# A fused attention and feed-forward kernel in fp32: first product by Strassen, one more product by two levels, a new order of the first two batches, and a list schedule of its own

## The chip, the cores and the metric

The kernel runs on one core of a Trainium2 chip. The metric is the device time of one execution in microseconds (us). The engines that matter here are TensorE (PE in the profile: matrix products into PSUM), VectorE (DVE), ScalarE (ACT), GpSimd (POOL[...]) and the DMA queues, most of which are fed by SyncE (SP). Every engine works through its own list of instructions in order and waits for others by semaphores.

## The reference, cut to what matters

There are 8 batches with 8 heads, 512 tokens and 32 state rows of width 64. Tokens attend to the state rows and the state rows to the tokens; both results together form 544 rows of width 512 per batch. They go through two matrix products with an ELU between them. The weights come in as float64.

```python
B, H, S, Ns, D = (8, 8, 512, 32, 64)
scores = scale * np.matmul(x, state.transpose(0, 1, 3, 2))      # tokens x state
a = softmax(scores);   xread = np.matmul(a, state)
scores2 = scale * np.matmul(state, x.transpose(0, 1, 3, 2))     # state x tokens
a2 = softmax(scores2); sread = np.matmul(a2, x)
...
h = x @ w_in                                                    # 512 -> 2048
g = np.where(h > 0.0, h, alpha * (np.exp(np.minimum(h, 0.0)) - 1.0))
return (g @ w_out).astype(np.float32)                           # 2048 -> 512
```

The kernel does not form `xread`. For a batch it forms m = (state rows times w_in), 256 x 2048, and then h = a m, so that the "first product" of a batch has an inner size of 256 instead of 512. The "second product" is g times w_out. The 256 state rows of all batches go through plain w_in at the end.

## The kernel before: the parts that matter

A batch's first product, plain: per block of 128 hidden columns two calls of 512 columns, then the ELU by two passes on ACT and one on DVE.

```python
def ffn1(b, fo):
    ps = bank(4 + fo % 2 if b == 0 else 3 + (fo + 1) % 3)
    for k in range(G):                       # G = 2
        matmul(ps, m_t[b, fo // 4][:, k, fo % 4 * P : (fo % 4 + 1) * P], st[b, k, "aT"],
               start=(k == 0), stop=(k == G - 1))
    return ps

def exp_part(ps):
    e = epool.tile([P, ps.shape[-1]], FP32, tag="e", name="e_sb")
    scalar.activation(out=e, in_=ps, func=AF.Relu, scale=-1.0)
    scalar.activation(out=e, in_=e, func=AF.Exp, scale=-1.0)
    return e

def max_part(fo, e, ps):                     # max(e - 1, h)
    vector.scalar_tensor_tensor(out=g_all[:, fo, : ps.shape[-1]], in0=e, scalar=-1.0, in1=ps,
                                op0=ALU.add, op1=ALU.max)
```

m is made by small matmuls on tiles of the array (64 rows, 32 columns each), 8 calls of 512 columns per chunk of 512 hidden columns; in batch 0 in halves of 256 columns.

The second product is done by Strassen's method (in Winograd's form: 7 products, here called P1 to P7, of blocks of half size) in batches 1 to 7 and for the state rows; P3, P4, P5 and P7 are again done so inside ("two levels", class `Second`) in batches 2 to 7, and P3 and P4 in batch 1. Batch 0 does it plainly.

```python
def ffn2_row(ps, fo):                        # batch 0
    for c in range(R):                       # R = 4
        matmul(ps[c], g_all[:, fo, c * P : (c + 1) * P], w_out[:, fo],
               start=(fo == 0), stop=(fo == FO - 1))
...
# class Strassen, steps(); two = self.second
product(0, self.a11, b11, after_p1, first=True)
product(1, self.a12, b21, after_p2, first=True, last=True)
product(0, self.s, t_w[2], after_p6, last=5 in two)          # P6, one level
if 7 in two:
    in_two(7, 2, (1, 1), after_p7, fresh=True)
...
used = {k: second[k] for k in (4, 3)}        # batch 1
```

The weights are converted from raw float64 words in 32 blocks, each by 3 passes on ACT and 4 on DVE. A written-out plan for batch 0 interleaves, block by block, the conversion of w_in, the conversion of w_out, the first product (`F`), the ELU (`R`, `E`) and the second product (`O`), and fills TensorE's early holes with products that nothing reads (`Z`):

```python
w:8.1 Z:8 sr:0 tt:0.0 src:0 w:2.2 Z:14 F:0 w:6.1 F:1 w:8.2 R:0 M:0.0.1 R:1 E:0 Mc:0.0.1
E:1 O:0 w:9.1 w:4.2 w:10.1 w:9.2 F:2 w:7.1 w:6.2 M:0.1.0 F:3 R:2 w:7.2 Mc:0.1.0 O:1
...
```

Of the kernel before, what the change touches and what calls it, by code (L numbers as in the profile page):

```python
# [17 lines left out]


# [3 lines left out]


@with_exitstack
def kernel(
# [8 lines left out]

# [14 lines left out]
    NRAW = 7  # L53
# [8 lines left out]
    w_in_v = moe_w_in.rearrange("(co ci) f -> ci co f", ci=P)  # L62
    w_out_v = moe_w_out.rearrange("(fo fi) c -> fi fo c", fi=P)

    def pool(name, bufs, **kw):
        return ctx.enter_context(tc.tile_pool(name=name, bufs=bufs, **kw))

    cpool = pool("const", 1)
    xpool = pool("x", 1)
    apool = pool("attn", 2)  # L70
    atpool = pool("aT", 2)
    mpool = pool("m", 3)
    work = pool("work", NRAW + 4)
    small = pool("small", 4)
    epool = pool("elu", 3)
    opool = pool("o", 2)
    wpool = pool("w2", 1)


    w_in_mem = pool("mem", 1, space=bass.MemoryType.DRAM).tile(  # L80
        [P, 2 * FC, NP, 256], FP32, name="w_in_mem"
    )
    psum = pool("ps", 1, space=PSUM).tile([P, 8, 512], FP32, name="ps")

    def bank(i):
        return psum[:, i]

    def pair(i):

        return psum[:, i : i + 2]  # L90

    class InOrder:
        def __init__(self, engine):
            self.engine, self.on = engine, True

        def __getattr__(self, name):
            def call(*args, **kw):
                ins = getattr(self.engine, name)(*args, **kw)  # L100
                return tc.keep_in_program_order(ins) if self.on else ins

            return call

    tensor, sync, vector, scalar, gpsimd = (
        InOrder(e) for e in (nc.tensor, nc.sync, nc.vector, nc.scalar, nc.gpsimd)
    )
    matmul = tensor.matmul

    def transpose(out, in_):  # L110


        for t in range(2):
            rows = slice(t * 64, (t + 1) * 64)
            tensor.transpose(out[:, t], in_[rows], ident[rows, rows], tile_position=(t * 64, 0))
# [4 lines left out]
    ident = cpool.tile([P, P], FP32, name="ident")  # L120

    w_in = cpool.tile([P, 2 * FC, NP, 256], FP32, name="w_in")
    w_out = cpool.tile([P, FO, DM], FP32, name="w_out")

    g_all = cpool.tile([P, FO, S], FP32, name="g_all")

    kT = cpool.tile([P, B, P], FP32, name="kT")

    read = cpool.tile([P, B, G, D], FP32, name="read")

    x_t, st, m_t = {}, {}, {}

    def load_x(b, engines):
        x_t[b] = xpool.tile([P, R, DM], FP32, name="x_sb")
        x_v = x[b].rearrange("h (p r) d -> p r h d", r=R)
        for r in range(R):
            engines[r % len(engines)].dma_start(
                out=x_t[b][:, r].rearrange("p (h d) -> p h d", d=D), in_=x_v[:, r]
            )

    def load_blocks(b):

        for i in range(2):
            st[b, "blocks", i] = raw = opool.tile([P, 2, R * P], FP32, tag="o", name="x_blocks")
            for j in range(2):
                for k in range(4):
                    x_v = x[b, 2 * (2 * i + j) + k // 2].rearrange(
                        "(q p r) d -> p r q d", q=P // 32, r=R  # L150
                    )
                    sync.dma_start(
                        out=raw[k * 32 : (k + 1) * 32, j].rearrange(
                            "p (r q d) -> p r q d", r=R, d=32
                        ),
                        in_=x_v[:, :, :, k % 2 * 32 : (k % 2 + 1) * 32],
                    )

    def turn_blocks(b, m):

        i, j = divmod(m, 2)
        if j == 0:
            st[b, "xT", i] = work.tile([P, 2, R * P], FP32, tag="w", name="xT_b")
        st[b, m] = st[b, "xT", i][:, j]
        vector.transpose(st[b, m], st[b, "blocks", i][:, j])

    state_v = state.rearrange("b (m c) n d -> c m n b d", c=G)

    def load_states(b0, b1, engines=None):

        shape = [P, b1 - b0, G, D]
        if b0 == 0:
            raw = cpool.tile(shape, FP32, name="s_first")
        else:
            raw = work.tile(shape, FP32, tag="w", name="s_sb")
        for c in range(G):
            if b0 == 0:
                engines[c % len(engines)].dma_start(out=raw[:, 0, c], in_=state_v[c, :, :, 0])
                continue
            for m in range(NP):  # L180
                sync.dma_start(
                    out=raw[m * NS : (m + 1) * NS, :, c], in_=state_v[c, m, :, b0:b1]
                )
        return raw

    def turn_states(raw, b0, b1):
        ps = st["k_ps"] = pair(6)[:, :, : (b1 - b0) * 64].rearrange("p t (b q) -> p t b q", q=64)
        for b in range(b1 - b0):
            transpose(ps[:, :, b], raw[:, b].rearrange("p c d -> p (c d)"))

    def copy_states(b0, b1):
        vector.tensor_copy(
            out=kT[:, b0:b1].rearrange("p b (t q) -> p t b q", t=2), in_=st["k_ps"]
        )

    def load_weights(src):
        _, n, k = src.shape
        raw = work.tile([P, n, k], moe_w_in.dtype, tag="w", name="raw")
        sync.dma_start(out=raw, in_=src)
        return raw  # L200

    def low_words(raw):
        return raw.bitcast(U32).rearrange("p n (j w) -> p n j w", w=2)[:, :, :, 0]

    def high_words(raw):
        return raw.bitcast(U32).rearrange("p n (j w) -> p n j w", w=2)[:, :, :, 1]

    def convert_1(dst, raw):

        lo, hi = low_words(raw), high_words(raw)

        scalar.activation(
            out=lo.bitcast(FP32), in_=lo, func=AF.Copy, scale=2.0**-29, bias=2.0**23
        )
        scalar.activation(out=lo, in_=lo.bitcast(FP32), func=AF.Copy, bias=-(2.0**23))


        scalar.activation(out=dst, in_=hi.bitcast(FP32), func=AF.Abs)  # L220

    def convert_2(dst, raw):
        lo, hi = low_words(raw), high_words(raw)
        vector.tensor_scalar(
            out=dst, in0=dst, scalar1=as_float(896 << 20),
            scalar2=as_float((1151 << 20) - 1), op0=ALU.max, op1=ALU.min,
        )

        bits = dst.bitcast(U32)
        vector.tensor_scalar(  # L230
            out=bits, in0=bits, scalar1=3, scalar2=0x3FFFFFF8,
            op0=ALU.logical_shift_left, op1=ALU.bitwise_and,
        )
        vector.scalar_tensor_tensor(
            out=bits, in0=hi, scalar=0xC0000000, in1=bits,
            op0=ALU.bitwise_and, op1=ALU.bitwise_or,
        )
        vector.tensor_tensor(out=bits, in0=bits, in1=lo, op=ALU.add)

    def load_w_in(c, k):  # L240

        h, n = divmod(k, 2)
        rows = slice(2 * n, 2 * n + 2)
        cols = slice(c * 512 + h * 256, c * 512 + (h + 1) * 256)
        return w_in[:, 2 * c + h, rows], load_weights(w_in_v[:, rows, cols])

    def load_w_out(fo):
        raw = load_weights(w_out_v[:, fo : fo + 1])
        return w_out[:, fo : fo + 1], raw

    def turn_x(b, i, first=6):

        ps = pair(first).rearrange("p t (j r q) -> p t j r q", j=2, q=64)
        for j in range(2):
            for r in range(R):
                m = 2 * i + j
                transpose(ps[:, :, j, r], x_t[b][:, r, m * P : (m + 1) * P])
        st[b, "xT", i] = ps

    def copy_x(b, i):  # L260
        xT = opool.tile([P, 2, R * P], FP32, tag="o", name="xT")
        for j in range(2):
            st[b, 2 * i + j] = xT[:, j]
            scalar.copy(
                out=xT[:, j].rearrange("p (r t q) -> p t r q", t=2, q=64),
                in_=st[b, "xT", i][:, :, j],
            )

    def by_state(b, rhs, first=6):


        ps = pair(first)
        _, j, n = rhs[0].shape
        for m in range(NP):
            for g in range(G):
                d = slice(g * D, (g + 1) * D)
                matmul(
                    ps[m * NS : (m + 1) * NS, g, : j * n].rearrange("p (j n) -> p j n", j=j),
                    kT[d, b, m * NS : (m + 1) * NS],
                    rhs[m][d],  # L280
                    start=True,
# [291 lines left out]

# [160 lines left out]

# [202 lines left out]
```

## Time and profile before

Three runs gave 747.8, 748.39 and 748.39 us, median 748.39. The profiled execution spans 744.4 us, at a granted TensorE clock of 1.000.

| What | Value |
|---|---|
| Start of batch 2 on TensorE | 213.84 us |
| Batches 2 to 6, each | about 79.6 us |
| Batch 7 (611.8 to 689.0) | 77.2 us |
| State rows to the end (689.0 to 744.4) | 55.4 us |
| POOL TENSOR_TENSOR, 128x512 | 1047 to 1063 ns each |
| ACT first pass of the ELU, 128x512 (from PSUM) | 597 ns each |
| DVE last pass of the ELU, 128x512 | 685 ns each |
| First matmul of a first product | 31.96 us |

In the profile a matmul call shows as two records. A line of the timeline gives the start, the length until the last of the group has ended, the engine, and the group of equal instructions; the next group may start before the last one has ended, so a rate is read from start to start. In the table of stretches the columns are the stretch, its length, the busy time and the number of instructions of PE, weight load, DVE, ACT and POOL, the granted clock, the DMA share and GB/s.

### The profile page before, as it was taken

The numbers are of one execution on the slowest core, as the hardware profiler recorded it, in microseconds if no ns is written. First come the engines' busy times: TensorE is split into PE (matmuls) and PEld (weight loads), VectorE is DVE, ScalarE is ACT, GpSimd is POOL, SyncE is SP. The second block draws the span as 40 slices with busy tenths as digits, with TensorE's granted clock in tenths as the row PEclk, the third lists the DMA queues.
The fourth block names the chain that finished last, engine by engine and source line by source line (L and its number), as shares of the span: only waits on it lengthen the run. The fifth ranks groups of instructions, "written<-read, shape, count | busy, mean of one in ns | idle before, by whom it ended". The sixth has DMA issues, their size and how long they took to land.

```text
span 744.4 us, 11377 instructions
## 1 busy us (share of the span) xinstructions
PE 723.7 (97%) x4472; PEld 502.5 (68%) x4472; DVE 486.0 (65%) x892; ACT 293.3 (39%) x539; POOL 34.4 (5%) x38
## 2 busy tenths in 40 slices
PE   4899999989999999999999999999999999999998
PEld 2544444348874798469944896479746894699886
DVE  2999975799437883677556864787367845556231
ACT  5899955542126311651055203621264106400420
POOL 0100002002000200010000200020002000000000
PEclk9999999999999999999999999999999999999999
DMA  9667900801634063503461164307340403003000
GB/s 282 225 201 239 326 0 1 167 4 22 177 94 133 5 179 84 160 1 106 122 153 46 26 173 110 116 13 187 83 144 1 143 33 137 1 1 142 29 4 25
DMA packets 126366, 76.25 MB, mean 102 GB/s; under 512 B 113768, under 2 KB 114280, under 8 KB 122472
## 3 DMA queue, kind: packets, MB, share of 16 engines
q1 hardware_dynamic: 124004, 74.90, 34.8%
q10 hardware_dynamic: 2308, 0.62, 0.4%
q8 instruction: 35, 0.57, 0.3%
q14 instruction: 19, 0.16, 0.1%
HBM read 59.24 MB, written 13.11 MB: 97 GB/s over the span
## 4 chain that ended last, share of the span: by engine, by line
PE 89%; DVE 6%; SPq 1%; DMA 1%; ACT 1%; issue 1%; POOL 0%; ACTq 0%; DVEq 0%; POOLq 0%
PE ps L100 89%; DVE w_in L100 2%; SPq L100 1%; DMA x_sb<-in_x_dram 1%; DVE g_all L100 1%; DVE total_t L100 0%; DVE s L100 0%; DVE top L100 0%; DVE w_out L100 0%; ACT e_sb L100 0%; POOL t_sb L100 0%; ACT xT L100 0%; DVE xT_b L100 0%; DVE aT L100 0%; DVE t_sb L100 0%
## 5 line engine op out<-in xcount | busy, mean ns | idle before, releaser
L100 PE MATMUL ps<-w_out,g_all 128*128 128x256 f32 (+2 forms) x1088 | 232.5, 366 | 1.1 <-DVE g_all L100 0.8
L100 PE MATMUL ps<-aT,m_sb 128*128 128x512 f32 x512 | 226.3, 595 | 1.1 <-DVE m_sb L100 0.8
L100 PEld LDWEIGHTS ps<-w_out,g_all 128*128 128x128 f32 x1088 | 176.6, 191 | 53.5 <-issue 37.1
L100 PEld LDWEIGHTS ps<-aT,m_sb 128*128 128x128 f32 x512 | 95.4, 190 | 122.0 <-issue 109.1
L100 ACT ACTIVATE e_sb<-ps 128x512 f32<-128x512 f32 (+1 forms) x144 | 82.5, 573 | 220.4 <-PE ps L100 205.1
L100 DVE SCALAR_TENSOR_TENSOR g_all<-e_sb,ps 128x512 f32<-128x512 f32 (+1 forms) x144 | 94.2, 656 | 101.0 <-ACT e_sb L100 100.4
L100 DVE TENSOR_TENSOR o_sb<-o_sb,ps 128x128 f32<-128x128 f32 (+2 forms) x170 | 52.6, 310 | 75.2 <-PE ps L100 73.5
L100 ACT ACTIVATE e_sb<-e_sb 128x512 f32<-128x512 f32 (+1 forms) x144 | 87.3, 606 | 4.6
L100 PE MATMUL ps<-t_w,s 128*128 128x256 f32 (+1 forms) x480 | 88.8, 339 | 0.0
L100 PEld LDWEIGHTS ps<-t_w,s 128*128 128x128 f32 x480 | 77.6, 191 | 8.1 <-DVE o_sb L100 0.2
L100 ACT COPY o_sb<-ps 128x512 f32<-128x512 f32 (+2 forms) x52 | 20.6, 424 | 151.7 <-PE ps L100 144.6
L100 ACT ACTIVATE raw<-raw 128x512 f32<-128x512 uint32 x64 | 43.7, 683 | 1.0
L100 DVE TENSOR_TENSOR s<-s,g_all 128x512 f32<-128x512 f32 (+1 forms) x36 | 32.2, 897 | 15.9 <-PE ps L100 15.5
L100 POOL TENSOR_TENSOR t_sb<-t_sb,top_t 128x512 f32<-128x512 f32 x16 | 16.7, 1047 | 517.0 <-DVE top_t L100 517.0
L100 DVE TENSOR_TENSOR g_all<-g_all,s 128x512 f32<-128x512 f32 (+1 forms) x36 | 32.1, 891 | 9.6 <-PE ps L100 9.6
L100 PE MATMUL ps<-w_in,kT 64*32 64x512 f32 (+1 forms) x576 | 34.0, 547 | 0.9 <-ACT a_s L100 0.9
L100 DVE TENSOR_TENSOR g_all<-g_all 128x512 f32<-128x512 f32 (+1 forms) x36 | 32.2, 894 | 0.5
L100 DVE TENSOR_TENSOR s<-g_all 128x512 f32<-128x512 f32 (+1 forms) x36 | 31.6, 883 | 0.8 <-DMA aT_s<-a_blocks 0.4
L100 PE MATMUL ps<-t_w,g_all 128*128 128x128 f32 (+1 forms) x240 | 32.1, 282 | 0.0
L100 PE MATMUL ps<-w_in,s 128*128 128x128 f32 x240 | 31.2, 277 | 0.0
L100 PEld LDWEIGHTS ps<-t_w,g_all 128*128 128x128 f32 x240 | 29.8, 192 | 0.5
L100 PEld LDWEIGHTS ps<-w_in,s 128*128 128x128 f32 x240 | 28.7, 192 | 0.6 <-DVE o_sb L100 0.5
(86 smaller groups left out, 557.1 us busy)
## 6 DMA issues: line engine op xcount, KB each, us to landing
w_in<-w_in_mem SPq DMA_DIRECT2D x26, 1024.0 KB, 5.9
raw<-in_moe_w_in_dram SPq DMA_DIRECT2D x16, 512.0 KB, 4.6
raw<-in_moe_w_out_dram SPq DMA_DIRECT2D x16, 512.0 KB, 4.5
out_dram<-o_sb SPq DMA_DIRECT2D x16, 512.0 KB, 2.8
x_sb<-in_x_dram SPq DMA_DIRECT2D x30, 256.0 KB, 4.9
x_blocks<-in_x_dram SPq DMA_DIRECT2D x96, 64.0 KB, 2.4
w_in_mem<-w_in SPq DMA_DIRECT2D x4, 1024.0 KB, 8.3
aT_s<-a_blocks SPq DMA_DIRECT2D x96, 32.0 KB, 1.9
```

What stands on the lines that cost most here:

```text
L100: ins = getattr(self.engine, name)(*args, **kw)
```

## The change

The kernel is rewritten. The instructions are first collected as operations with their tiles and an estimated cost; a list schedule then orders each engine's instructions, picks PSUM banks (six that rotate, two fixed), and places filler products in TensorE's holes during the first 40 us of its own estimate. The operations themselves differ in these points:

1. The first product of batches 2 to 7 is done by Strassen's method, chunk by chunk (`ffn1_chunk`): 7 products of half blocks instead of 8, to save TensorE work. The sums of the blocks of m and of a (`sum_m`, `sum_a`) are done by POOL, and results move between banks by ACT and DVE.
2. P6 of batches 2 to 7 is done by two levels, and P5 and P7 of batch 1 too; batch 0 gets Strassen's method with one level.
3. m is always made in halves of 256 columns, and both w_in buffers of the old kernel give way to three half buffers, refilled from DRAM.
4. Batches 0 and 1: all of w_in is converted first and used for both batches' m; both first products run, w_out is converted meanwhile, and then the second products of both follow, interleaved.
5. The ELU is ACT exp, POOL min(e, 1) - 1, DVE max with h, instead of ACT, ACT, DVE. A conversion of a block is 2 passes on ACT and 4 on DVE.

```diff
+    def sum_m(m):
+
+        l11, l12, l21, l22 = m_blocks(m)
+        s1, s2, s4 = (m[:, 1024 + 256 * i : 1280 + 256 * i] for i in range(3))
+        Q.tensor_tensor(out=s1, in0=l21, in1=l22, op=ALU.add)
+        Q.tensor_tensor(out=s2, in0=s1, in1=l11, op=ALU.subtract)
+        Q.tensor_tensor(out=l21, in0=l11, in1=l21, op=ALU.subtract)
+        Q.tensor_tensor(out=s4, in0=l12, in1=s2, op=ALU.subtract)
...
+        A.activation(out=e, in_=ps, func=AF.Exp)
+        Q.tensor_scalar(
+            out=e, in0=e, scalar1=1.0, scalar2=1.0, op0=ALU.min, op1=ALU.subtract
+        )
+        V.tensor_tensor(out=to, in0=e3, in1=view, op=ALU.max)
...
+        def part_1():
+            two(pa, l11, r11, True)
+            A.copy(out=pb, in_=pa)
+            two(pc, s1, t1, True)
+            two(pb, s2, t2, False)
+            two(pa, l12, r21, False)
+            A.copy(out=u2, in_=pb)
+            elu(pa, g_to[:, k0, lo], e[0])
+            two(pb, s3, t3, False)
+            A.copy(out=u3, in_=pb)
+
+        def part_2():
+            two(pb, l22, t4, False)
+            V.tensor_tensor(out=pa, in0=u3, in1=pc, op=ALU.add)
+            elu(pb, g_to[:, k1, lo], e[1])
+            two(pc, s4, r22, False)
+            elu(pa, g_to[:, k1, hi], e[2])
+            V.tensor_tensor(out=pc, in0=u2, in1=pc, op=ALU.add)
+            elu(pc, g_to[:, k0, hi], e[3])
...
+        for hc in range(8):
+            for r in range(2):
+                n = 2 * hc + r
+                convert(*blocks[n])
+                read_block(n + 6)
...
+            make_m(0, hc, w)
+            copy_m_half(0, hc, m_sb[:, c % 2])
+            make_m(1, hc, w)
...
+            if hc % 2:
+                ffn1_plain(0, c, g0, a_sb, e_slots)
+        for c in range(FC):
+            ffn1_plain(1, c, g_sb, aT1, e_slots)
+            for n in range(16 + 4 * c, 20 + 4 * c):
+                convert(*blocks[n])
...
+            second[6].sums(o.s, s_2[0], m_sb[:, 1, :1024])
+            combine(o.a12, o.a12, o.s)
...
+            steps = second[6].steps(c12)
```

`two` is a product of half blocks: two calls of 256 columns. V is DVE, A is ACT, Q is POOL.

## The prediction

> **What bounds the kernel now.** I read the busy table and the chain first, then the engines' busy time by stretch, TensorE's timeline of one batch, and the first 32 us of all engines.
>
> ```profile
> PE 723.7 (97%) x4472; PEld 502.5 (68%) x4472; DVE 486.0 (65%) x892; ACT 293.3 (39%) x539; POOL 34.4 (5%) x38
> PE 89%; DVE 6%; SPq 1%; DMA 1%; ACT 1%; issue 1%; POOL 0%; ACTq 0%; DVEq 0%; POOLq 0%
> ```
>
> TensorE is 97% busy and 89% of the chain that ended last. Only fewer TensorE columns, or less idle TensorE, can move the end much. Stretches next: length, then busy time of PE, weight load, DVE, ACT, POOL.
>
> ```profile
> 0.00:32.00 32.00, 18.95 (x211) 14.57 (x211) 18.09 (x38) 22.17 (x40) 5.10 (x10) 1.00 0.79 248
> 32.00:128.70 96.70, 95.91 (x470) 40.83 (x471) 80.87 (x152) 75.13 (x131) 4.15 (x4) 1.00 0.50 163
> 452.70:532.20 79.50, 79.50 (x529) 57.46 (x528) 53.17 (x99) 26.44 (x49) 4.19 (x4) 1.00 0.38 100
> ```
>
> Batch 5 (452.7 to 532.2) is TensorE work from end to end with DVE at 67%. Batch 0 (32 to 128.7) is nearly the same for TensorE, but DVE is at 84%: it converts weights there. So there are two regimes, and the change touches both. TensorE in batch 4's second product, and in batch 5's first:
>
> ```profile
> 408.98 10.63 PE L100 MATMUL ps<-w_out,g_all 128*128 128x256 f32 x48
> 419.45 7.07 PE L100 MATMUL ps<-t_w,s 128*128 128x256 f32 x32
> ...
> 428.14 1.06 PE L100 MATMUL ps<-w_in,s 128*128 128x128 f32 x8
> 429.03 1.06 PE L100 MATMUL ps<-w_out,g_all 128*128 128x128 f32 x8
> ...
> 452.69 10.46 PE L100 MATMUL ps<-aT,m_sb 128*128 128x512 f32 x24
> 463.09 1.95 PE L100 MATMUL ps<-w_in,kT 64*32 64x512 f32 x32
> 464.96 17.43 PE L100 MATMUL ps<-aT,m_sb 128*128 128x512 f32 x40
> ```
>
> Each matmul call leaves two records. From start to start: a 512-column call takes 17.27/20 = 0.864 us (464.96 to 482.23, where the next group starts), a 256-column call 10.47/24 = 0.436 (408.98 to 419.45), a 128-column call 0.893/4 = 0.223 (428.14 to 429.03). Small calls cost almost nothing extra, which is what makes Strassen worth while.
>
> **The Trainium skill.** "TensorE: Matmul & The Clock Gate", section "Back-to-back issue gap", has the warm gap as N/2.4 + 2.5 ns. Four such gaps make 0.863, 0.437 and 0.223 us for 512, 256 and 128 columns: the trace agrees for all three, so a call costs four. "SBUF — State Buffer", section "Who interferes with whom", says that GpSimd and VectorE share a port pair with an exclusive lock, taken by VectorE operations with two SBUF inputs and by its two-port forms. The trace agrees:
>
> ```profile
> 23.62 1.59 DVE L100 TENSOR_SCALAR w_in<-w_in 128x512 f32<-128x512 f32 x2
> 23.63 1.30 POOL L100 TENSOR_TENSOR t_sb<-t_sb,total_t 128x512 f32<-128x512 f32 x1 [3.77 <-DVE total L100]
> ...
> 42.11 0.88 DVE L100 TENSOR_SCALAR w_in<-w_in 128x512 f32<-128x512 f32 x2
> ```
>
> The DVE pair takes 1.59 us beside GpSimd and 0.88 without it. "GPSIMD Engine Reference", section "Engine selection", puts one-input GpSimd work at roughly line rate and two-input work at about 2x slower. The trace has only the second: 1.05 us against DVE's 0.685.
>
> **The change part by part.**
>
> First product of batches 2 to 7. Each of 4 chunks of hidden columns was 8 calls of 512 columns, 27.67 us a batch (10.40 + 17.27). Now it is 7 products of 2 calls of 256: 56 x 0.436 = 24.4. Minus 3.25.
>
> P6 by two levels. 16 calls x 0.431 = 6.90 us (419.45 to 426.35) become 28 x 0.2234 = 6.26. Minus 0.64.
>
> Making m in halves. Eight tiled calls of 512 columns take about 0.93 us (1.87 for 16). In batch 0 the half-width groups take 0.59 (42.40 to 42.99) where half would be 0.465. Now all are half width, sometimes two groups in a row; I take 0.5 to 0.55 each, 8 a batch, plus 0.3.
>
> A full batch: 79.5 - 3.25 - 0.64 + 0.3 = 75.9.
>
> Waits within the new first product. A product is copied from one bank to another by ACT (0.58 us plus about 0.2 to start) while one 0.87 us product runs, and a bank is written again only after the ELU has read it. The schedule is static and interleaves the next chunk, but margins are a tenth of a microsecond. I allow 0.5 us a batch: 76.4. The other engines have room. DVE: 53.2 + 4.7 (P6's sums and adds) + 5.4 (8 adds on banks) - 3.8 (m copies, now ACT) - 0.7 = 59 of 76 us. POOL: 4.2 + 16 one-input passes, estimated at 0.6, + 20 half-size sums, estimated at 0.55 from 1.05 = 25 us. ACT loses the ReLU pass (16 x 0.597 a batch) and gains copies.
>
> So batches 2 to 6 cost 5 x 76.4 = 382.0. Batch 7 with no successor was 77.2 (611.8 to 689.0) and becomes 77.2 - 3.9 + 0.15 + 0.5 = 73.95. The state rows, 55.4 us, keep their calls.
>
> Batches 0 and 1. Before, batch 2 starts at 213.84. TensorE saves: batch 0's second product was 64 x 0.864 = 55.3 us and is now 7 x 16 x 0.435 = 48.7 (minus 6.6); batch 1 takes two levels for P7 and P5 also (minus 1.3). But the order changes: all of w_in is converted first, both first products run, and batch 0's second product waits for w_out. The instruction order shows that before P6 of batch 0 DVE must do: 32 block conversions x 2.25 us (42.11 to 44.36) = 72; 32 ELU maxima x 0.66 = 21; two softmaxes at about 7.5 (4 transposes, 6 reductions at 0.6 to 0.65, small ones) = 15; 4 block transposes 2.6; 8 differences of 1024 elements x 1.15 = 9.2; copies 1.1. Sum 121. It starts near 12.7 as before, so P6 cannot start before 134. TensorE alone would reach P6 at 131: 105 us of work (110.7/2 = 55.3 first products, 28 for four Strassen products, 16 half-groups at 0.55, 13 for turns, scores and reads), 14 us before it can start, 12 us of hole while the softmax runs. DVE is thus the bound, and port conflicts come on top: 32 new GpSimd passes of about 0.6 and 8 of 1.05 lie beside conversions that use the shared port. One cost 0.7 above; the order puts operations without the port between them, so I add 3 rather than 16. P6 at 137. After it: 6 x 6.95 + 4 x 6.26 + 4.1 (scores, 4 half-groups, a read) = 70.9, so batch 2 starts near 207.9: a gain of only 6.
>
> Sum: 207.9 + 382.0 + 73.95 + 55.4 = 719.3 span, plus 4.0 between span and device time (748.39 - 744.4) = 723.
>
> **Rivals.**
>
> TensorE stays the bound everywhere. Then the beginning takes 131 + 70.9 = 202 and a batch 75.9, and the time is about 714. For it: batches 2 to 7 have no idle TensorE today and the list schedule orders all engines at once. Against it: the DVE sum above.
>
> DVE and POOL become the bound by the shared port. POOL goes from 4.2 to some 25 us a batch, and in the second product DVE has about 43 us in 50, much of it on two SBUF inputs. If a third of POOL's time delayed the chain, a batch would return to 79 to 82 and the beginning would take 215 to 220: about 745 to 755. For it: the 1.59 against 0.88. Against it: the sums have half a stage to arrive in.
>
> The beginning is bound by transfers. w_in (8.4 MB as raw words), x, and the write of the converted w_in fall together, about 14 MB before batch 0's last chunk. At the first stretch's 248 GB/s that is 57 us, and my DVE chain wants the last block at about 70. It would add 5 us at most.
>
> **Range and chances.** The batch is well known from columns; half a microsecond there is 3 us in total. The beginning is uncertain by 8 either way, and unforeseen waits mostly lengthen. 723 with 709 to 737. The 2% line is 733.4, below which most of the range lies: faster 0.83, within 2% 0.14, slower 0.03.
>
> **What would show it.** A batch period of 76 to 77 with TensorE full; call times of 0.436 in the first product. Batch 2's start at 200 to 216, with TensorE idle before P6 of batch 0 or before batch 0's last chunk, released by DVE. ReLU gone from ACT, POOL near 200 us in all. Wrong if TensorE shows gaps of over 1 us in each batch released by POOL or DVE, or if the beginning has no hole that DVE released.

## The result, and the profile after

The changed kernel takes 851.41 us (849.55 to 852.33, four runs) against 748.1 beside it: a ratio of 1.1375, 95% interval 1.1359 to 1.1391. It is 13.7% slower where I had predicted 3.4% faster.

The busy table and the chain of waits of the changed kernel, to set beside those of before:

```profile
PE 760.8 (89%) x5604; PEld 605.9 (71%) x5604; DVE 533.8 (63%) x982; ACT 245.8 (29%) x488; POOL 392.0 (46%) x294
PE 33%; DVE 24%; POOL 22%; issue 8%; DMA 6%; SPq 4%; ACT 3%; POOLq 0%; ACTq 0%; DVEq 0%
```

TensorE is no longer the chain: 33% instead of 89%. POOL went from 34.4 to 392.0 us of work, not to the 200 that I had put down. Over the whole run no engine is saturated, yet POOL and DVE hold 46% of the chain: it passes from engine to engine. The stretches (length, then busy PE, weight load, DVE, ACT, POOL, clock, DMA share, GB/s): the first 32 us, from there to the start of batch 1's second product (139.2 us), batch 4's first product (with the start of its second), and the whole of batch 4:

```profile
0.00:32.00 32.00, 30.10 (x289) 25.12 (x290) 17.93 (x43) 17.88 (x36) 4.82 (x10) 1.00 0.79 217
32.00:139.20 107.20, 94.12 (x596) 47.10 (x596) 81.22 (x155) 61.55 (x122) 66.62 (x36) 0.94 0.63 191
414.70:463.55 48.85, 38.21 (x211) 28.34 (x210) 21.71 (x32) 17.63 (x32) 36.41 (x24) 0.97 0.34 87
414.70:510.00 95.30, 82.57 (x666) 68.39 (x666) 59.40 (x111) 25.66 (x51) 50.42 (x40) 0.98 0.32 84
```

A batch takes 95.3 us (79.5 before, 76.4 predicted), and the first-product part has POOL busy for 36.4 of 48.9 us. The groups of that part name it (mean duration in ns, idle time of the engine before them, and what ended it):

```profile
L410 POOL TENSOR_SCALAR xe<-xe 128x512 f32<-128x512 f32 x16 | 30.9, 1944 | 22.4 <-ACT xe L410 22.4
L410 PE MATMUL ps<-aT,m 128*128 128x256 f32 x84 | 21.9, 401 | 7.6 <-DVE ps L410 4.2 <-ACT sec L410 3.4
L410 DVE TENSOR_TENSOR g<-xe,ps 128x512 f32<-128x512 f32 x16 | 11.0, 685 | 21.2 <-POOL xe L410 21.2
L410 ACT ACTIVATE xe<-ps 128x512 f32<-128x512 f32 x16 | 9.2, 598 | 20.1 <-DVE ps L410 17.4 <-POOL xe L410 1.3 <-PE ps L410 1.1
```

One GpSimd pass of the ELU takes 1.94 us on average. From batch 2 on its shortest, middle and longest durations are (min/median/max; the 32 passes of batches 0 and 1 have the same shortest and middle ones):

```profile
L410 POOL TENSOR_SCALAR xe<-xe x104: 1912/1918/2468, 229.2 to 822.9; 128x512 f32<-128x512 f32 x104
```

The minimum is as long as the median, so the pass itself is slow, and conflicts over the shared port add little to it: its mean is 1.951. DVE waits for POOL, the bank stays occupied, DVE's next sum onto the bank and ACT's exponential after it come late, the copy that TensorE needs stands behind that exponential in ACT's list, and TensorE waits for the copy. The chain of waits in the middle of batch 4, in order of time, shows it from piece to piece (start, length, what):

```profile
435.30 3.81 POOL xe L410 x2
...
439.14 0.69 DVE g L410
439.82 0.62 DVE ps L410
...
440.53 0.04 ACT xe L410
...
441.02 0.59 ACT sec L410
...
441.75 4.11 PE ps L410 x12
```

TensorE's own timeline over the same time:

```profile
436.30 2.86 PE L410 MATMUL ps<-aT,s 128*128 128x256 f32 x12
441.75 1.10 PE L410 MATMUL ps<-aT,s 128*128 128x256 f32 x4 [2.59 <-ACT sec L410]
442.68 1.45 PE L410 MATMUL ps<-aT,m 128*128 128x256 f32 x4
443.93 1.91 PE L410 MATMUL ps<-aT,s 128*128 128x256 f32 x4
445.63 1.49 PE L410 MATMUL ps<-aT,m 128*128 128x256 f32 x4
```

The 2.59 us gap was released by ACT, but the chain shows that ACT had waited for DVE, and DVE for POOL. Over the run TensorE waits most for these (for whom; total, times, longest):

```profile
PE ps L410 <- ACT sec L410: 31.0, 16, 2.6
PE ps L410 <- DVE ps L410: 21.9, 22, 2.5
PE ps L410 <- DVE o L410: 14.1, 21, 3.7
```

Four records that take 0.87 us elsewhere take 1.70 here (443.93 to 445.63): the granted clock from 444 to 447 was 0.57, and over the run 0.967 against 1.000 before. TensorE thus lost time to the clock too. Which gaps lower the clock is not shown: from 450 to 458 TensorE was busy for only 4.5 of 8 us, at a clock of 1.00.

### The profile page after: what moved, and what is told of

Its sections match the earlier page's. It is cut to its first block, busy times and chain, and to the rows that moved or that the text cites. A ratio compares the mean times of both kernels' runs of the same rounds, so it can differ in the third digit from the quotient of the medians.

```text
span 850.5 us, 14223 instructions
## 1 busy us (share of the span) xinstructions
PE 760.8 (89%) x5604; PEld 605.9 (71%) x5604; DVE 533.8 (63%) x982; ACT 245.8 (29%) x488; POOL 392.0 (46%) x294
## 4 chain that ended last, share of the span: by engine, by line
PE 33%; DVE 24%; POOL 22%; issue 8%; DMA 6%; SPq 4%; ACT 3%; POOLq 0%; ACTq 0%; DVEq 0%
PE ps L410 32%; POOL xe L410 15%; DVE g L410 6%; POOL sec L410 4%; DVE sec L410 4%; SPq L410 4%; DVE s L410 3%; DVE small L410 3%; DVE o L410 2%; DMA out_dram<-o 2%; DVE ps L410 2%; ACT xe L410 1%; DMA t_w<-in_moe_w_out_dram 1%; POOL s L410 1%; DMA o<-in_x_dram 1%
## 5 line engine op out<-in xcount | busy, mean ns | idle before, releaser
L410 POOL TENSOR_SCALAR xe<-xe 128x512 f32<-128x512 f32 x104 | 201.4, 1951 | 198.0 <-ACT xe L410 198.0
L410 PE MATMUL ps<-aT,m 128*128 128x256 f32 (+1 forms) x568 | 161.3, 424 | 43.6 <-ACT sec L410 21.1
L410 PE MATMUL ps<-w_out,g 128*128 128x256 f32 (+1 forms) x960 | 178.1, 336 | 1.3 <-DVE g L410 1.2
L410 DVE TENSOR_TENSOR g<-xe,ps 128x512 f32<-128x512 f32 x104 | 71.3, 685 | 158.1 <-POOL xe L410 157.9
L410 PEld LDWEIGHTS ps<-aT,m 128*128 128x128 f32 x568 | 105.5, 196 | 90.1 <-issue 44.8
L410 PEld LDWEIGHTS ps<-w_out,g 128*128 128x128 f32 x960 | 152.3, 193 | 22.7 <-ACT o L410 4.2
L410 PE MATMUL ps<-sec 128*128 128x128 f32 x544 | 74.6, 281 | 6.6 <-DVE o L410 6.5
L410 POOL TENSOR_SCALAR sec<-sec 128x512 f32<-128x512 f32 x32 | 62.4, 1973 | 29.5 <-ACT sec L410 29.5
L410 PEld LDWEIGHTS ps<-sec 128*128 128x128 f32 x544 | 66.9, 194 | 10.5 <-DVE o L410 10.1
L410 PE MATMUL ps<-t_w,s 128*128 128x128 f32 (+1 forms) x448 | 70.1, 308 | 1.1 <-DVE o L410 1.1
L410 ACT COPY o<-ps 128x128 f32<-128x128 f32 (+2 forms) x55 | 21.8, 408 | 120.6 <-PE ps L410 120.6
L410 ACT COPY m<-ps 128x512 f32<-128x512 f32 (+1 forms) x56 | 26.8, 529 | 48.9 <-PE ps L410 48.8
```

The lines of the kernel that those rows point to most:

```text
L410: ins = getattr(engine, name)(**{k: resolve(v) for k, v in kw.items()})
```

## The experiments

Three readings serve all of them: where batch 2 begins on TensorE's timeline, the period of a batch (from one batch's first product to the next), and the whole time. The period is that of the middle batches or the mean of all; in e1 it is 82.8 and 83.0 for batches 4 and 5, but the first is 87.4 and the mean of five is 84.4. In e5 batch 3 begins part of its first product early, so the first period is 72.0 and the other four are 79.1. All but e9 start from the changed kernel; the list schedule plans each version anew, so an edit of one operation also moves others.

| Run | Time, us | Ratio to before (95%) | Batch 2 starts | Period |
|---|---|---|---|---|
| before | 748 | | 213.8 | 79.5 |
| changed | 851.4 | 1.1375 [1.1359, 1.1391] | 224.7 | 95.3 |
| e1_act_elu | 761.8 | 1.0212 [1.0153, 1.0271] | 206.8 | 82.9 |
| e2_true_cost | 835.8 | 1.1166 [1.1118, 1.1215] | 247.4 | 91.8 |
| e3_min_only | 816.0 | 1.0901 [1.0858, 1.0944] | 222.8 | 90.0 |
| e4_min_add | 851.2 | 1.1372 [1.1339, 1.1404] | 224.7 | 94.9 |
| e9_before_pool | 774.1 | 1.0358 [1.0334, 1.0382] | 226.6 | 82.1 |
| e6_plain_first | 741.5 | 0.9920 [0.9904, 0.9937] | 204.9 | 80.5 |
| e8_plain_true | 747.9 | 1.0003 [0.9991, 1.0016] | 211.0 | 80.7 |
| e5_true_all | 737.0 | 0.9866 [0.9843, 0.9888] | 210.9 | 79.1 |
| e7_sp_cost | 737.1 | 0.9858 [0.9844, 0.9873] | 206.8 | 80.0 |
| e10_p6_one | 734.6 | 0.9829 [0.9811, 0.9847] | 209.8 | 78.4 |
| e11_p6_one_lag | 736.2 | 0.9840 [0.9819, 0.9862] | 212.2 | 78.6 |
| e12_late_lag | 731.5 | 0.9776 [0.9758, 0.9794] | 207.0 | 78.7 |

### e1: the ELU without GpSimd

```diff
-        A.activation(out=e, in_=ps, func=AF.Exp)
-        Q.tensor_scalar(
-            out=e, in0=e, scalar1=1.0, scalar2=1.0, op0=ALU.min, op1=ALU.subtract
-        )
-        V.tensor_tensor(out=to, in0=e3, in1=view, op=ALU.max)
+        A.activation(out=e, in_=ps, func=AF.Relu, scale=-1.0)
+        A.activation(out=e, in_=e, func=AF.Exp, scale=-1.0)
+        V.scalar_tensor_tensor(
+            out=to, in0=e3, scalar=-1.0, in1=view, op0=ALU.add, op1=ALU.max
+        )
```

> The changed kernel with the ELU of the kernel before (ACT ReLU, ACT exp, DVE add and max); nothing of the ELU on POOL, the list schedule plans anew. Theory A, the GpSimd pass of the ELU costs 1.92 us where I estimated 0.6 and paces the first products: batch period 76 to 78, batch 2 starts at 205 to 214, TensorE clock back to 1.00, time 715 to 730. Rival B, the GpSimd block sums (0.73 us each, 20 a batch) and the bank hand-overs pace the first product: period stays above 85, time above 780. Rival C, DVE and the shared port pace: DVE waits stay, time 760 to 800.

761.84 us: 89.6 us of the 103 came back by moving one pass. Batch 2 starts at 206.79, as theory A said (207.9 in the prediction). But the period is 82.9 and the time misses A's range by 32 us. The time lies inside C's range, so it is the waits that decide about C: those of TensorE for DVE fall from 48.5 us in all to 12.0. B said over 85 and over 780. B and C are thus rejected as the main cause; something else remains. e1's waits of TensorE over the run (engine and tile, for whom; total, times, longest), followed by its transfer queue in batch 4:

```profile
PE ps L410 <- DMA w_half<-w_in_mem: 10.4, 5, 2.6
PE ps L410 <- DVE o L410: 5.1, 5, 1.1
PE ps L410 <- DVE ps L410: 4.2, 7, 1.4
```

```profile
423.51 11.64 SPq L410 DMA_DIRECT2D xr<-xr  x16
435.25 5.02 SPq L410 DMA_DIRECT2D w_half<-w_in_mem  x4
```

TensorE now waits for a half of w_in. Its transfer stands in the queue behind 16 small ones, and SyncE takes 11.64/16 = 0.73 us for each, pauses between them included (the record of one issue is 0.61 in the middle of 96, that of a half of w_in 0.33); the schedule had reckoned 0.06 for every transfer. In the changed kernel this wait is not among TensorE's waits; it came up once GpSimd's pass was gone.

### e2, e3, e4: is it the work, the estimate, or the kind of operation

e2 changes only the schedule's estimates of GpSimd:

```diff
-                    cost = 0.08 + (1.9 if len(wide) > 1 else 1.0) * n
+                    cost = 0.40 + 1.27 * n if len(wide) > 1 else 0.08 + 3.59 * n
```

> The changed kernel with nothing altered but the schedule's estimates for GpSimd: 1.92 us for the ELU pass, 0.73 and 1.05 for the two-input sums of 256 and 512 elements. If the work itself is too much (theory A: 4 x 1.92 + 4 x 0.73 = 10.6 us of POOL a chunk against 6.1 of TensorE), it gains little: 825 to 850. If it is a schedule misled by wrong estimates, other work can be put beside it and the time falls below 780.

835.84 us, inside the first range: with right estimates the same work is still 12% slower than before. The wrong estimate by itself was worth about 16 us, as the net of two: the period falls to 91.8, but batch 2 starts at 247.4, 22.7 us later. So right estimates gave a better order for the batches and a worse one for the beginning.

e3 leaves one operation in the GpSimd pass and puts the -1 into DVE's:

```diff
-        Q.tensor_scalar(
-            out=e, in0=e, scalar1=1.0, scalar2=1.0, op0=ALU.min, op1=ALU.subtract
-        )
-        V.tensor_tensor(out=to, in0=e3, in1=view, op=ALU.max)
+        Q.tensor_scalar(out=e, in0=e, scalar1=1.0, scalar2=None, op0=ALU.min)
+        V.scalar_tensor_tensor(
+            out=to, in0=e3, scalar=-1.0, in1=view, op0=ALU.add, op1=ALU.max
+        )
```

> The GpSimd pass does one operation (min with 1); the subtraction goes into the last DVE pass. If a pass costs by its arithmetic operations, it falls to about 1.0 us and the time to 735 to 765; if a one-input pass has a fixed rate whatever it computes, it stays 1.9 us and the time at 845 to 855.

```profile
L410 POOL TENSOR_SCALAR xe<-xe x104: 1480/1486/2036, 227.3 to 789.1; 128x512 f32<-128x512 f32 x104
```

Neither answer was right: 1.486 us for one operation, 1.918 for two, so the second costs 0.43; if the first costs as much, an estimate, some 1.05 is there without any. The time falls to 815.96. Taking 0.43 us from 136 passes (58.8 us in all) shortened the kernel by 35 us, about 60% of it: most of what a pass costs lies on the path.

e4 writes the same pass as min and add of -1:

```diff
-            out=e, in0=e, scalar1=1.0, scalar2=1.0, op0=ALU.min, op1=ALU.subtract
+            out=e, in0=e, scalar1=1.0, scalar2=-1.0, op0=ALU.min, op1=ALU.add
```

> The same GpSimd pass with min and add of -1 in place of min and subtract of 1. Theory A has no opinion; if subtract is the slow operation, the pass falls towards 0.6 to 1.0 us and the time below 770; if not, 1.9 us and 845 to 855.

851.19 us and the same pass time: subtract is not the slow one.

### e9: the GpSimd pass alone, in the kernel before

```diff
-        scalar.activation(out=e, in_=ps, func=AF.Relu, scale=-1.0)
-        scalar.activation(out=e, in_=e, func=AF.Exp, scale=-1.0)
+        scalar.activation(out=e, in_=ps, func=AF.Exp)
+        gpsimd.tensor_scalar(
+            out=e, in0=e, scalar1=1.0, scalar2=1.0, op0=ALU.min, op1=ALU.subtract
+        )
...
-        vector.scalar_tensor_tensor(
-            out=g_all[:, fo, : ps.shape[-1]], in0=e, scalar=-1.0, in1=ps,
-            op0=ALU.add, op1=ALU.max,
-        )
+        vector.tensor_tensor(out=g_all[:, fo, : ps.shape[-1]], in0=e, in1=ps, op=ALU.max)
```

> The kernel before with one thing changed: its ELU as in the changed kernel (ACT exp, GpSimd min and subtract, DVE max). Theory A: the pass takes 1.92 us against 1.73 of TensorE for a block, so batches 0 to 7 are paced by GpSimd in the first product: period up from 79.5 to 84 to 88, time 775 to 810. If the pass is hidden in the old order (only the new form suffers): 745 to 760.

774.14 us. The pass slows the old kernel too, by 26 us: batch 2 starts 12.8 later and the period grows to 82.1, less than I expected. Its groups on GpSimd, with the length for 256 elements too:

```profile
L100 POOL TENSOR_SCALAR e_sb<-e_sb 128x512 f32<-128x512 f32 x128 | 246.9, 1954 | 301.4 <-ACT e_sb L100 301.2
L100 POOL TENSOR_SCALAR e_sb<-e_sb 128x256 f32<-128x256 f32 x16 | 17.8, 1113 | 55.7 <-ACT e_sb L100 55.7
```

The same pass costs 2.6 us a batch there and 95.3 - 82.9 = 12.4 in the changed kernel. In the plain form TensorE meets one ELU per 1.73 us of work, and the pass (1.92) is only slightly slower. In the Strassen form a chunk holds four passes and four block sums, 4 x 1.92 + 4 x 0.73 = 10.6 us of POOL against 14 x 0.436 = 6.1 of TensorE, and a bank must have left its ELU before the next sum is put there. That the order of dependencies makes the rest of the difference is read from the chain shown above; no run separates it from POOL's added sums.

### e6, e8, e5, e7: what Strassen in the first product is worth

e6 makes the first product of batches 2 to 7 plain again, in e1:

```diff
-            sum_a()
...
-            sum_m(m_to[0])
...
-        p[0] = ffn1_chunk(b, 0, g_sb)
-        p[0][0]()
-        p[1] = ffn1_chunk(b, 1, g_sb)
-        p[0][1]()
+        slots = [xe[:, i * 512 : (i + 1) * 512] for i in range(4)]
+        ffn1_plain(b, 0, g_sb, a_sb, slots)
         make_m(b, 4, st["w", 4])
```

> e1_act_elu with the first product of batches 2 to 7 plain again (two calls of 512 columns, no sums of m and a); P6 by two levels, the order of batches 0 and 1 and the ELU as there. If Strassen's waits cost more than its 3.25 us of columns, the period falls below 82.9, to 79 to 82, and the time to 738 to 758. If it pays for itself, the period rises to 84 to 86 and the time to 765 to 780.

741.51 us: with the schedule's old estimates, Strassen loses. e5 is e1 with its remaining estimates set to the traces (e2's line, and these):

```diff
-            queue, 0.06, issue(
+            queue, 0.72, issue(
...
-        return 0.0 if a.engine == b.engine and a.engine != SP else self.LATENCY[a.engine]
+        if a.engine == b.engine and a.engine != SP:
+            return 0.0
+        return self.LATENCY[a.engine] + (0.25 if b.engine == PE else 0.0)
```

> The ELU of the kernel before (as in e1_act_elu), and the schedule's other estimates set to what the traces show: 0.72 us for each transfer that SyncE issues (it had 0.06), 0.73 us for GpSimd sums of 256 elements, and 0.25 us more before a TensorE product that waits for another engine. Theory: the 82.9 us batch of e1_act_elu is 75.9 of columns plus waits that the schedule did not know of (transfer queue 2.1, P6's chain 1.0, bank hand-overs some 3): batch period 77 to 80, time 728 to 745. Rival: the hand-overs are inherent to the chunked Strassen form, the period stays 81 to 83 and the time 750 to 760.

e8 puts the same estimates into e6:

> Plain first product (e6_plain_first) with the estimates of e5_true_all. Columns say 79.2 us a batch; period 79.5 to 81 and 735 to 745 in all. Against e5_true_all it gives the net worth of Strassen in the first product when the schedule knows its costs: e5 faster by 5 to 18 if the saving survives, slower if not.

e5 takes 736.95 us, e8 747.86. With equal estimates Strassen in the first product is thus worth 11 us, a period of 79.1 against 80.7: it saves half of its 3.25 us of columns. e8 missed its range because of the beginning (211.0 against e6's 204.9), not the batch. The best plain run is therefore e6, with the old estimates, and against it e5 gains 4.6 us. A plain first product with the later changes of e10 and e12 was not run. e7 corrects only the transfer queue, in e1:

```diff
-            queue, 0.06, issue(
+            queue, 0.72, issue(
```

> e1_act_elu with only the transfer queue's estimate corrected (0.72 us for each transfer issued by SyncE, it had 0.06). If the queue's wait is all that this estimate changes: the 2.1 us wait of TensorE for a fetched half of w_in goes, period 80.5 to 81, time 745 to 752, and the larger part of e5_true_all's gain came from the hand-over estimate. If the time is 735 to 742, the queue did it all.

737.05 us, and no wait of TensorE for a half of w_in is left: this one number brought 24.8 us, all that e5 brought. TensorE's waits for that transfer were only 10.4 us in e1; the rest came with the new order, and no run takes it apart. The other two estimates of e5, for hand-overs and GpSimd's sums, shorten a batch further (79.1 against 80.0) but cost 4 us in the beginning (210.9 against 206.8), and the two effects cancel.

Where e5's batch stands to the old one, from TensorE's timeline, start to start by kind of call:

| us in a batch | before | changed | e1 | e5 | e10 |
|---|---|---|---|---|---|
| first product | 27.67 | 32.35 | 26.66 | 24.84 | 24.75 |
| m and scores | 4.61 | 9.76 | 7.81 | 6.03 | 5.59 |
| second product | 46.21 | 52.13 | 47.29 | 47.24 | 46.73 |

A gap is counted with the calls ahead of it; turns and reads, 1.03 us in each, are left out. In e5 the first product nearly has its predicted saving (24.84, 24.4 predicted). But m in halves costs 1.4 us more than before instead of 0.3, and the second product with P6 by two levels takes 1.0 us more instead of 0.64 less.

### e10, e11, e12: P6, and a faster kernel

e10 is e5 with P6 of batches 2 to 7 at one level:

```diff
-            A.copy(out=c12, in_=x1)
+            A.copy(out=c11, in_=x1)
...
-            o.product(x1, o.a12, b21, False)
-            A.copy(out=c11, in_=x1)
-            second[6].sums(o.s, s_2[0], m_sb[:, 1, :1024])
+            y = o.open()
+            o.product(y, o.a12, b21, True)
+            o.plus(y, 0, 0)
...
-            steps = second[6].steps(c12)
+            o.product(x1, o.s, t_w[2], False)
+            A.copy(out=c12, in_=x1)
+            A.copy(out=c21, in_=x1)
```

> e5_true_all with P6 of batches 2 to 7 back at one level (P1 held in its bank, P6 added there). Columns say it costs 0.65 us a batch more. In e5_true_all the second product took 47.2 us a batch against 46.2 before, so I expect the two-level P6 to lose by its adds and hand-overs: period 77.8 to 78.6, time 729 to 735. If the columns decide: 739 to 743.

734.56 us and a period of 78.4. By the traces a batch with a successor loses 0.7 us through the second level, and batches 2 to 7 together take 466.1 us against 468.8. By time the intervals of e5 and e10 overlap a little (0.9843 to 0.9888, 0.9811 to 0.9847), so the loss is not shown by time alone. This wait of TensorE for DVE's adds in e5 is absent in e10:

```profile
PE ps L412 <- DVE o L412: 6.6, 10, 0.8
```

e11 is e10 with 0.10 for the hand-over in place of 0.25:

> As e10_p6_one, with 0.10 us in place of 0.25 for a product that waits for another engine. If the real cost of such a hand-over is near 0.25: slower than e10_p6_one by 3 to 10. If the larger figure only spoils the order in the first 200 us (batch 2 started at 210.9 in e5_true_all and 206.8 in e1_act_elu): faster by 2 to 5.

736.23 us, within the noise of e10: between 0.10 and 0.25 nothing is decided. e12 keeps 0.25, but only for what comes after the first two batches' shared part:

```diff
-        return self.LATENCY[a.engine] + (0.25 if b.engine == PE else 0.0)
+        return self.LATENCY[a.engine] + (0.25 if b.engine == PE and b.number >= self.mark else 0.0)
...
     o, x1 = start()
+    plan.mark = len(plan.ops)
```

> e10_p6_one, with the 0.25 us for hand-overs to TensorE counted only in what follows the first two batches' own work. e7_sp_cost, without it, began batch 2 at 206.8, e10_p6_one at about 209.8; e10_p6_one's batch is 78.4 against 80.0. If both can be had together: batch 2 at 206.5 to 208, period 78.4, time 729 to 733. If the order of the first two batches changes for another reason: 734 to 737.

731.47 us, 2.2% faster than before: batch 2 at 206.97, a period of 78.7. Its busy table, and the stretches before P6 of batch 0 and of batch 4:

```profile
PE 720.7 (99%) x5462; PEld 592.7 (81%) x5462; DVE 507.2 (69%) x917; ACT 318.4 (44%) x624; POOL 137.6 (19%) x158
32.00:135.00 103.00, 99.37 (x655) 57.41 (x654) 95.07 (x175) 78.40 (x155) 4.16 (x4) 0.98 0.60 188
363.87:442.67 78.80, 78.80 (x643) 67.01 (x642) 55.82 (x101) 34.40 (x67) 21.40 (x24) 1.00 0.40 101
```

TensorE is 99% busy again. With POOL out of the ELU the beginning is close to two limits at once: TensorE 99.4 and DVE 95.1 of 103 us.

## Why the prediction was wrong, point by point

**The step that failed** is the sum for POOL in the working of a full batch: "16 one-input passes, estimated at 0.6". The trace of before held no one-input GpSimd pass of that size, and I took 0.6 from the Trainium skill's page "GPSIMD Engine Reference", section "Engine selection", which calls one-input work roughly line rate. The measurement is 1.918 us for min and subtract, 1.486 for min alone, and it decides. With it the sum for POOL in a chunk is 10.6 us against 6.1 of TensorE, and the sentence "The other engines have room" falls. The sum was also taken over the wrong stretch: over a batch it would still have shown room with the right figure, 4.2 + 16 x 1.92 + 20 x 0.73 = 49.5 of 76 us (50.4 of 95.3 measured). What failed is the first product, where POOL was busy for 36.4 of 48.9 us and each pass stands between a bank and its next use. The prediction's own sign of being wrong, gaps of over 1 us released by DVE or POOL, is there: the 22 waits for DVE's sums are up to 2.5 us. e1, e3 and e9 show the cause from three sides: the pass removed, made shorter, and put alone into the old kernel.

**The rival** that named POOL was there, but for another mechanism: port conflicts, at 745 to 755. DVE's sums of 1024 elements still took 1.22 us. Port conflicts may be seen in longer records, 18 of the 136 passes by over 5% and some block sums (0.728 in the middle, 0.858 in the mean for those of m), but all of POOL's records together exceed the middle ones of their kind by only 16 us of its 392. The right rival would have been "POOL's pass is as slow per element as its two-input one or slower".

**The waits** "I allow 0.5 us a batch" were the second mis-sized term. In e1, without the pass, they are 82.9 - 75.9 = 7 us in the middle batches, 8.5 in the mean. The estimate for the transfer queue was the larger part: I had checked the volume of transfers, not the time in which SyncE issues them, although before had 96 + 96 small ones, at 0.6 us each by their records. e7 removes 2.9 us of the middle period, 4.4 of the mean, and 24.8 of time. With all estimates right e5 still has 3.2 us.

**P6 by two levels** was put at minus 0.64 and costs about 0.7 (e10): 28 calls form 7 small products, and each of these ends in an add by DVE. **m in halves** was put at plus 0.3 and costs 1.4 in e5, 1.0 in e10.

**The beginning**: 207.9 predicted, 224.7 measured, 206.8 in e1. P6 of batch 0 on TensorE, in the changed kernel and in e1:

```profile
153.02 7.07 PE L410 MATMUL ps<-t_w,s 128*128 128x256 f32 x32
135.09 7.07 PE L410 MATMUL ps<-t_w,s 128*128 128x256 f32 x32
```

With the pass it starts 16 us after the predicted 137. TensorE had waited for DVE for 9.9 us between 32 and 140, while DVE waited for POOL's passes for 21.8. From P6 to batch 2 it is 71.7 us in both runs (70.9 predicted). In e1 P6 starts 1.9 us before the predicted time, but TensorE had no hole there; it lost about 4 us earlier, in three waits of 0.5 to 2.0 us around 52 to 62, which ACT released. DVE is a limit beside TensorE, not ahead of it. So the predicted start holds without the pass, its reason only in part, and the close agreement is partly luck.

**What held**: the call times of 0.436 and 0.223 us; the last batch (73.95 predicted, 74.06 in e1, though 94.4 in the changed kernel); the state rows (55.4 predicted, 55.5 in e1).

The miss of 128.4 us thus divides into 89.6 for the pass (changed to e1), 24.8 for the transfer queue (e1 to e7), and 14 for the smaller waits (e7 to 723). The division holds for this order of edits: each run is planned anew, and e2 shows that some 16 of the 89.6 came back with the estimate alone.

## What to carry to other kernels

Before work is moved to an idle engine, measure that very operation in that size there: a pass missing from the trace is a hole in the prediction, and a static schedule's plan can lose much by one wrong constant (24.8 us here for the transfer queue). Right constants do not ensure a better plan, though: with those of GpSimd alone e2's beginning grew by 22.7 us, and with all of e5's the plain form was 6.4 us slower (e8 against e6). Check the load of an engine stage by stage, not over a batch. Count the issue time of small transfers as well as their bytes, and expect the next wait to appear only when the first is gone. A saving in columns is paid out only as far as the hand-overs between engines allow: here Strassen gave half of it in the first product, and none at the second level of P6.

## What the runs showed of the hardware that I had not expected

- A GpSimd TENSOR_SCALAR of 128x512 in fp32 took 1.918 us with two operations and 1.486 with one, longer than a TENSOR_TENSOR of the same size (1.05). DVE's TENSOR_SCALAR of that size took 0.42 in the trace before.
- GpSimd TENSOR_TENSOR took 0.728 us for 256 elements and 1.05 for 512. By a straight line through the two, an estimate, a good 0.4 us of it does not depend on the size.
- SyncE took 0.73 us for each of 16 small transfers between SBUF places, one after another, and 0.33 us by the record to issue a half of w_in of 512 KB.
- The run with many gaps of TensorE had a lower granted clock on a single core: 0.967 in the mean and 0.57 over 3 us, against 0.998 in e12. What sets it is not shown.
